# Key, query and feature projections of a linear attention layer on 64-row halves of TensorE, in a two-layer kernel

## The chip, the cores and the metric

The kernel runs on one NeuronCore of a Trainium2 chip. The metric is the device time of one execution in microseconds (us); lower is better. A profile is one profiled execution, with a record of every instruction of the engines: TensorE (PE, its weight loads as PEld), VectorE (DVE), ScalarE (ACT), GpSimd (POOL) and SyncE (SP), and of the DMA queues.

## The reference

Linear attention with exponential features, followed by a gated MLP with a spatial mixing matrix. Batch 8, 8 heads, 576 tokens, head dimension 64, 128 features (256 with both signs), model width 512, 1024 hidden.

```python
def phi(x):
    proj = np.einsum('bhsd,df->bhsf', x, w_phi)
    proj = proj - np.max(np.abs(proj), axis=-1, keepdims=True)
    return np.concatenate([np.exp(proj), np.exp(-proj)], axis=-1)
q_p, k_p = phi(q), phi(k)
kv = np.einsum('bhsf,bhsd->bhfd', k_p, v)
z = np.sum(k_p, axis=2)
num = np.einsum('bhsf,bhfd->bhsd', q_p, kv)
den = np.einsum('bhsf,bhf->bhs', q_p, z)[..., None] + 1e-06
x = (num / den)            # then tokens x (heads * head_dim)
h = np.maximum(x @ w_in, 0.0)
u, v = h[..., :512], h[..., 512:]
v_n = (v - mean(v)) / np.sqrt(var(v) + 1e-06)
v_s = np.einsum('ts,bsd->btd', w_spatial, v_n) + b_spatial[None, :, None]
out = (u * v_s) @ w_out
```

## The kernel before

**Units.** Of each batch's 576 tokens, 512 are handled as four blocks of 128 and the last 64 as a tail. A *pair* unit is two heads of one batch (8 blocks of 128 tokens by 64 dimensions); a *tail* unit is the 64 last tokens of all heads for two batches. There are 36 units, numbered `i` from 0: four pair units a batch, and one tail unit for each two batches (units 1, 9, 18 and 27). Batches 2 to 7 begin at units 10, 14, 19, 23, 28 and 32.

**What a unit needs.** The transposed inputs `kT` and `qT` have 128 partitions: two blocks of 64 dimensions on top of each other, so four columns groups `j` with two blocks each. For the first batches TensorE transposes them (L225); from batch 2 on SP does it by DMA for a whole batch (`cross`, tiles `kT_b` and `qT_b`). The weight `wphi2` is 128 x 256 with w_phi in rows 0 to 63 of its left half and again in rows 64 to 127 of its right half, zeros elsewhere.

- `by_token` (L229 to 234) projects: one matmul of 256 columns gives two blocks, since the zeros of `wphi2` keep them apart. `a_keys` reduces to the absolute maximum `mk` on DVE (L244) and evacuates exp(p) and exp(-p) into `kf` on ACT (L247). `a_queries` takes only the maxima `mq` (L258), which POOL (DVE in the first five units) splits into a high and a low bf16 part, `mhl`.
- `a_scale` makes exp(-mk) and exp(mk) (`em`, ACT L267) and POOL multiplies v by them (`vs`, L272).
- `a_max_t` transposes `mhl` on TensorE and DVE copies 16 rows to `mT` (L294).
- `a_qfeat` (L296 to 322) projects q once more with features on the partitions (L304), subtracts the maxima by a matmul with `sel`, a matrix of -1 (L308), and ACT evacuates exp(p) and exp(-p) into `qf` (L321). For tail units the two lines are L313 and L315.
- `a_kv` sums `kf` times `vs` over tokens (L334, L336), `a_num` multiplies `qf` by the sums (L354) and `norm` divides (L344, L345), giving `x`. `tail_num` does it for tails (L382), with 64 output columns of the array. `a_x_t` transposes `x` into `xT`, by DMA from SP for most units (L363).

**The gMLP.** When a batch's last unit is through, `b_tasks` puts its matrix products into `queue`: `b_v` (L403, evacuated by ACT, statistics on DVE), `b_ln` (normalizing on POOL, L413 to L420), `b_u` (L456), `b_s` (L477, L478), `b_o` (L500, with the store by SP). A task is four or five matmuls of 512 columns, and its cost is given in us.

**The order.** It is written out by hand. `step(i)` goes through `ORDER`, and each entry works on the unit whose lag to the step is listed; after each entry `fill` adds `RATE` times the entry's share to a credit (at most `CAP`) and takes tasks from the queue as long as half the next one's cost is covered. Before: keys and queries of unit i, attention of unit i-3, sums of unit i-2, inputs of unit i+1, features of unit i-2, `x` of unit i-4, maxima of unit i-1. The shares sum to 1.0 and `RATE` is 3.12. After each step come the loads and DMA transposes that `at` lists: k five steps ahead of a batch's first unit and q and v four steps ahead, `cross` two steps ahead (`AT, AB, XP = 4, 5, 2`). What is left in the queue after the last step is run then.

All PSUM tiles share one pool of 8 banks, and a framework sets the banks and the semaphores.

Of the kernel before, what the change touches and what calls it, by code (L numbers as in the profile page):

```python
# [8 lines left out]
FP32 = mybir.dt.float32  # L9
BF16 = mybir.dt.bfloat16  # L10
AF = mybir.ActivationFunctionType
# [5 lines left out]
def kernel(  # L17
# [42 lines left out]
    def pin(start):  # L60
        return lambda *a, **kw: tc.keep_in_program_order(start(*a, **kw))
# [72 lines left out]
    for i in range(NM):  # L134
        for tiles, name in ((mhl, "mhl"), (mT, "mT")):
# [1 line left out]
            pin(nc.vector.memset)(t, 0.0)  # L137
            tiles.append(t)

    sel1 = cpool.tile([P, H], BF16)  # L140
    sel = cpool.tile([P, H, F], BF16)
    pin(nc.vector.tensor_tensor)(out=sel1, in0=ident[:, 0:H], in1=ident[:, H:2 * H], op=ALU.add)
    pin(nc.vector.tensor_scalar)(out=sel, in0=sel1.unsqueeze(2).to_broadcast([P, H, F]), scalar1=-1.0,
                                 scalar2=None, op0=ALU.mult)
    for x in ("k", "q"):
        pin(nc.vector.tensor_copy)(out=st[0][x][:, 0:2], in_=first[x])
# [79 lines left out]
            u[x + "T"] = a1.tile([P, 4, P], BF16, tag=x + "T", name=x + "T", bufs=2 if x == "k" else 4)  # L226
            copy(out=u[x + "T"], in_=pt)

    def by_token(xT, half):  # L229
        ps = psum.tile([P, 4, F], FP32, tag="bank", name="ps")  # L230
        for x in range(2):
            nc.tensor.matmul(out=ps[:, 2 * x:2 * x + 2, :], lhsT=xT[:, 2 * half + x, :], rhs=wphi2,  # L232
                             start=True, stop=True)
        return ps

    def a_keys(u):

        u["mk"] = small.tile([P, H], FP32, tag="mk", name="mk")
        u["kf"] = feat.tile([P, 2, H, F], BF16, tag="kf" if u["pair"] else "kf_t", name="kf",
                            bufs=4 if u["pair"] else 2)  # L240
        for half in range(2):
            pk = by_token(u["kT"], half)
            hs = slice(4 * half, 4 * half + 4)
            nc.vector.tensor_reduce(out=u["mk"][:, hs], in_=pk, axis=AX.X, op=ALU.max,  # L244
                                    apply_absolute_value=True)
            for s, sc in ((0, 1.0), (1, -1.0)):
                nc.scalar.activation(out=u["kf"][:, s, hs, :], in_=pk, func=AF.Exp, bias=0.0, scale=sc)  # L247

    def a_queries(u):

        m, early = mhl[u["i"] % NM], u["i"] < EARLY
        if not early:
            mq = small.tile([P, H], FP32, tag="mq", name="mq")
        for half in range(2):
            pq = by_token(u["qT"], half)
            if early and half == 0:
                mq = pq[:, 0, 0:H]
            nc.vector.tensor_reduce(out=mq[:, 4 * half:4 * half + 4], in_=pq, axis=AX.X, op=ALU.max,  # L258
                                    apply_absolute_value=True)
        eng = nc.vector if early else nc.gpsimd  # L260
        eng.tensor_copy(out=m[:, 0:H], in_=mq)
        eng.tensor_tensor(out=m[:, H:2 * H], in0=mq, in1=m[:, 0:H], op=ALU.subtract)

    def a_scale(u):
        em = small.tile([P, 2, H], FP32, tag="em" if u["pair"] else "em_t", name="em", bufs=3 if u["pair"] else 1)
# [25 lines left out]
    def a_max_t(u):  # L291
        pt = psum.tile([P, P], BF16, tag="bank", name="pt")
        nc.tensor.transpose(out=pt, in_=mhl[u["i"] % NM], identity=ident)
        nc.vector.tensor_copy(out=mT[u["i"] % NM][0:2 * H, :], in_=pt[0:2 * H, :])  # L294

    def a_qfeat(u):  # L296

        m = mT[u["i"] % NM]
        u["qf"] = []
        for half in range(2):  # L300
            pq = psum.tile([P, 4, P], FP32, tag="bank", name="pq")
            if u["pair"]:
                for par in range(2):
                    nc.tensor.matmul(out=pq[:, 2 * par:2 * par + 2, :], lhsT=wphi2[:, par * F:(par + 1) * F],  # L304
                                     rhs=u["qT"][:, 2 * half:2 * half + 2, :], start=True, stop=False)
                    for x in range(2):
                        j = 4 * half + 2 * x + par
                        nc.tensor.matmul(out=pq[:, 2 * par + x, :], lhsT=sel[:, j, :], rhs=m,  # L308
                                         start=False, stop=(x == 1))
            else:  # L310
                for x in range(4):
                    h = 4 * half + x
                    nc.tensor.matmul(out=pq[:, x, :], lhsT=wphi2[:, (h % 2) * F:(h % 2 + 1) * F],  # L313
                                     rhs=u["qT"][:, h // 2, :], start=True, stop=False)
                    nc.tensor.matmul(out=pq[:, x, :], lhsT=sel[:, h, :], rhs=m, start=False, stop=True)  # L315
            if u["pair"]:
                qf = feat.tile([P, 2, 4, P], BF16, tag="qf", name="qf", bufs=7)
            else:
                qf = feat.tile([P, 2, 4, P], BF16, tag="qf_t", name="qf_t", bufs=4)
            for s, sc in ((0, 1.0), (1, -1.0)):  # L320
                nc.scalar.activation(out=qf[:, s], in_=pq, func=AF.Exp, bias=0.0, scale=sc)  # L321
            u["qf"].append(qf)

    def a_kv(u):
        d, dg, bl = st[u["b"]], gs[u["g"]], u["b"] % 2
# [21 lines left out]
    def a_num(u):  # L347
        d = st[u["b"]]
        u["x"] = a1.tile([P, NB, 2, D], BF16, tag="x", name="x", bufs=3)
        for hh in range(2):  # L350
            pn = psum.tile([P, NB, DA], FP32, tag="bank", name="pn")
            for pos in range(NB):
                for s in range(2):
                    nc.tensor.matmul(out=pn[:, pos, :], lhsT=u["qf"][hh][:, s, pos, :],  # L354
                                     rhs=d["kv"][:, 2 * u["pj"] + hh, s, :], start=(s == 0), stop=(s == 1))
            norm(pn, u["x"][:, :, hh, :])

# [13 lines left out]
    def tail_num(g, bls):  # L371
        d = gs[g]
        qf = d["unit"]["qf"]
        if "xt" not in d:
            d["xt"] = a1.tile([P, H, D], BF16, tag="xt", name="xt")
        for i in range(2):
            pn = psum.tile([P, 4, DA], FP32, tag="bank", name="pn")
            for y in range(4):
                for bl in bls:
                    r = slice(bl * TL, (bl + 1) * TL)  # L380
                    for s in range(2):
                        nc.tensor.matmul(out=pn[r, y, :], lhsT=qf[i][:, s, y, r],  # L382
                                         rhs=st[2 * g + bl]["kv"][:, 4 * i + y, s, :],
                                         start=(s == 0), stop=(s == 1))
            r = slice(bls[0] * TL, (bls[-1] + 1) * TL)
            norm(pn, d["xt"][r, 4 * i:4 * i + 4, :], r)
# [142 lines left out]
    def unit(i):  # L529
        return units[i] if 0 <= i < NU else None  # L530
# [3 lines left out]
    def b_tasks(b):  # L534
# [15 lines left out]
        if tail:  # L550
# [5 lines left out]
            for x in bls:  # L556
                ts += [(mm, lambda j=j, x=x: b_o(2 * g + x, j)) for j in range(NB)]
        return ts

    ORDER = (("keys", 0.375), ("queries", 0.25), ("attention", 0), ("sums", 0.25),  # L560
             ("next", 0.125), ("features", 0), ("out", 0), ("maxima", 0))
    RATE = 3.12
    CAP = 2.11
    LAGS = dict(next=-1, maxima=1, features=2, sums=2, attention=3, out=4)
    FIRST = dict(next=-1, maxima=1, features=2, sums=2, attention=3, out=3)
    credit = [0.0]

    def fill(share):
# [3 lines left out]
            task()  # L572
            credit[0] -= cost

    FT = dict(next=-1, maxima=1, features=2)

    def lag(u, what):
        return (FT if u["i"] == 1 else FIRST if u["pair"] and u["b"] == 0 else LAGS).get(what, 0)

    def step(i):  # L580

        if i == 0:
            a_transpose(units[0])
        for what, share in ORDER:
            for u in units[max(0, i - 5):i + 2]:
                if u["i"] + lag(u, what) != i or (what in ("sums", "attention", "out") and not u["pair"]):
                    continue
                last = u["pair"] and u["pj"] == NP - 1
                if what == "keys":
                    a_keys(u)  # L590
                    a_scale(u)
                elif what == "sums":
                    a_kv(u)
                elif what == "queries":
                    a_queries(u)
                elif what == "next":
                    a_transpose(u)
                elif what == "maxima":
                    a_max_t(u)
                elif what == "out":  # L600
                    a_x_t(u)
                    if last:
                        finish_batch(u, tail_x_t)
                        queue.extend(b_tasks(u["b"]))
                elif what == "features":
                    a_qfeat(u)
                elif what == "attention":
                    a_num(u)
                    if last:
                        finish_batch(u, tail_num)  # L610
            fill(share)

    def finish_batch(u, f):
        g, bl = u["g"], u["b"] % 2
        if g in SPLIT:
            f(g, [bl])
        elif bl == 1:
            f(g, [0, 1])
# [65 lines left out]
```

## Time and profile before

| what | value |
|---|---|
| median of 8 runs | 292.56 us (287.19 to 295.39) |
| the profiled execution | 291.43 us |
| its span, first to last instruction | 289.6 us |
| granted TensorE clock | 0.993 |
| PE busy (L334 and L354, 512 matmuls each, 66 columns) | 264.1 us, 91% |
| ACT busy (kf 144 and qf 144 instructions of 128x512) | 229.4 us, 79% |
| DVE busy | 201.9 us, 70% |
| POOL busy | 181.8 us, 63% |
| DMA | 40.31 MB, mean 139 GB/s |

How to read it: busy time is the union of an engine's instructions, so overlapping ones count once. The duration of a matmul is modelled and reaches into the next one's; the distance between the starts of two of them is what one costs. A group line gives the source line, engine, operation, tiles (out<-in) and shape, the count, busy us and mean ns of one, and after the second bar the idle time of the engine before these instructions and what ended it. A slice row cuts the span into 40 equal parts with the busy share of each in tenths.

### The profile page before, as it was taken

What the parts mean: (1) busy time and instruction counts of PE and PEld (TensorE: products, weight loads), DVE (VectorE), ACT (ScalarE), POOL (GpSimd) and SP (SyncE); (2) the same over time, 40 slices, a digit from 0 to 9 for tenths busy, and PEclk for the clock granted to TensorE, in tenths of its full rate; (3) what the DMA queues carried; (4) which work ended last, traced back from release to release, by engine and by line L of the source; (5) the groups of instructions that cost most, each with busy time, mean ns of one, the idle gap of its engine ahead of it and who ended that gap; (6) DMA issues with size and microseconds to landing.
All of it is one profiled execution on the core that took longest, in us unless ns stands there. A gap on an engine that the chain in (4) does not pass through costs nothing.

```text
span 289.6 us, 7965 instructions
## 1 busy us (share of the span) xinstructions
PE 264.1 (91%) x3070; PEld 179.4 (62%) x3070; DVE 201.9 (70%) x509; ACT 229.4 (79%) x517; POOL 181.8 (63%) x320
## 2 busy tenths in 40 slices
PE   3188899999999999889999999989999999999984
PEld 2067676776766766557667677656677777545441
DVE  6289997968868697377696987568697854454610
ACT  7658998899799988599999779789999756566033
POOL 8349998896337996748689964844969700058300
PEclk9999999999999999979999999999999999999999
DMA  7979999948377699997974999999311003600037
GB/s 202 225 126 158 210 232 206 173 141 107 48 169 155 180 149 127 168 242 157 119 122 91 215 131 157 228 301 247 57 22 20 18 2 91 238 3 0 0 85 243
DMA packets 81706, 40.31 MB, mean 139 GB/s; under 512 B 50242, under 2 KB 77058, under 8 KB 81668
## 3 DMA queue, kind: packets, MB, share of 16 engines
q1 hardware_dynamic: 54180, 28.32, 44.3%
q0 software_dynamic: 27328, 11.41, 34.7%
q8 instruction: 24, 0.39, 0.6%
q14 instruction: 14, 0.11, 0.1%
q10 hardware_dynamic: 160, 0.07, 0.1%
HBM read 32.85 MB, written 9.44 MB: 146 GB/s over the span
## 4 chain that ended last, share of the span: by engine, by line
PE 58%; ACT 16%; DVE 11%; DMA 10%; POOL 2%; issue 2%; ACTq 0%; SPq 0%; POOLq 0%; DVEq 0%
PE pv L403 10%; PE ps L477 8%; PE pu L456 7%; PE po L500 6%; ACT qf L321 5%; DMA out_dram<-ob 5%; ACT kf L247 5%; PE ps L232 5%; PE pv L334 4%; PE pn L354 4%; DMA q_tl<-in_q_dram 4%; PE pq L308 3%; PE pq L304 3%; DVE mk L244 3%; ACT ob L502 2%; PE ps L478 2%
## 5 line engine op out<-in xcount | busy, mean ns | idle before, releaser
L247 ACT ACTIVATE kf<-ps 128x512 bf16<-128x512 f32 x144 | 77.2, 680 | 6.7 <-DVE mk L244 6.5
L272 POOL TENSOR_TENSOR vs<-v_f,em 128x512 bf16<-128x512 f32 x64 | 65.5, 1047 | 22.5 <-ACT em L267 21.6
L321 ACT ACTIVATE qf<-pq 128x512 bf16<-128x512 f32 x128 | 67.9, 665 | 8.5 <-PE pq L308 8.5
L244 DVE TENSOR_REDUCE mk<-ps 128x4 f32<-128x512 f32 x72 | 46.1, 677 | 0.7 <-PE ps L232 0.2
L258 DVE TENSOR_REDUCE mq<-ps 128x4 f32<-128x512 f32 x62 | 39.9, 680 | 4.0 <-PE ps L232 2.6
L502 ACT COPY ob<-po 128x512 f32<-128x512 f32 (+1 forms) x37 | 21.7, 606 | 23.9 <-PE po L500 16.2
L406 DVE BATCH_NORM_STATS2 stats<-vr 128x6 f32<-128x512 bf16 (+1 forms) x37 | 24.8, 688 | 20.2 <-ACT vr L405 20.0
L477 PE MATMUL ps<-w_spT,vn 128*128 128x512 bf16 x128 | 32.8, 379 | 0.0
L403 PE MATMUL pv<-w_in_bf,xT 128*128 128x512 bf16 x128 | 32.0, 386 | 0.5 <-DVE mT L294 0.5
L456 PE MATMUL pu<-xT,w_in_bf 128*128 128x512 bf16 x128 | 31.5, 379 | 0.0
L480 DVE TENSOR_TENSOR uT<-ps,uT 128x512 bf16<-128x512 f32 x32 | 22.0, 688 | 12.7 <-PE ps L478 11.5
L500 PE MATMUL po<-w_out_bf,uT 128*128 128x512 bf16 x128 | 30.4, 379 | 0.0
L308 PE MATMUL pq<-mT,sel 128*128 128x128 bf16 x256 | 30.0, 219 | 0.0
L308 PEld LDWEIGHTS <-sel 128*128 128x128 bf16 x256 | 25.0, 98 | 3.9
L405 ACT ACTIVATE vr<-pv 128x512 bf16<-128x512 f32 (+1 forms) x37 | 22.8, 672 | 4.2 <-PE pv L403 4.1
L354 PEld LDWEIGHTS <-qf 128*128 128x128 bf16 x512 | 20.8, 98 | 8.5 <-issue 1.9
L345 DVE TENSOR_TENSOR x<-pn,rc 128x256 bf16<-128x256 f32 x64 | 25.0, 418 | 0.5
L334 PE MATMUL pv<-vs,kf 128*128 128x66 bf16 x512 | 24.9, 195 | 0.2 <-ACT kf L247 0.2
L420 POOL TENSOR_SCALAR vn<-vr,rs 128x512 bf16<-128x512 bf16 x32 | 24.2, 773 | 0.8
L354 PE MATMUL pn<-kv,qf 128*128 128x66 bf16 x512 | 22.7, 195 | 1.3 <-ACT qf L321 1.2
L334 PEld LDWEIGHTS <-kf 128*128 128x128 bf16 x512 | 22.1, 98 | 1.8 <-issue 1.0
L304 PE MATMUL pq<-qT_b,wphi 128*128 128x256 bf16 x96 | 22.4, 273 | 0.0
(120 smaller groups left out, 530.2 us busy)
## 6 DMA issues: line engine op xcount, KB each, us to landing
v_f<-in_v_dram SPq DMA_DIRECT2D x8, 1024.0 KB, 8.6
out_dram<-ob SPq DMA_DIRECT2D x32, 256.0 KB, 4.0
k_bf<-in_k_dram POOLq DMA_DIRECT2D x7, 512.0 KB, 7.3
q_bf<-in_q_dram POOLq DMA_DIRECT2D x7, 512.0 KB, 8.2
v_tl<-in_v_dram SPq DMA_DIRECT2D x8, 128.0 KB, 6.6
w_in_bf<-in_moe_w_in_dram POOLq DMA_DIRECT2D x2, 512.0 KB, 7.9
out_dram<-ob SPq DMA_DIRECT2D x8, 128.0 KB, 2.4
k_tl<-in_k_dram POOLq DMA_DIRECT2D x8, 64.0 KB, 6.7
```

Of the source, the lines that this page charges most:

```text
L244: nc.vector.tensor_reduce(out=u["mk"][:, hs], in_=pk, axis=AX.X, op=ALU.max, apply_absolute_value=True)
L247: nc.scalar.activation(out=u["kf"][:, s, hs, :], in_=pk, func=AF.Exp, bias=0.0, scale=sc)
L258: nc.vector.tensor_reduce(out=mq[:, 4 * half:4 * half + 4], in_=pq, axis=AX.X, op=ALU.max, apply_absolute_value=True)
L272: nc.gpsimd.tensor_tensor(out=vs[:, s, :, 0:D], in0=st[u["b"]]["v"][:, pj * H:(pj + 1) * H, :], in1=em[:, s, :].unsqueeze(2).to_broadcast( ...
L308: nc.tensor.matmul(out=pq[:, 2 * par + x, :], lhsT=sel[:, j, :], rhs=m, start=False, stop=(x == 1))
L321: nc.scalar.activation(out=qf[:, s], in_=pq, func=AF.Exp, bias=0.0, scale=sc)
L334: nc.tensor.matmul(out=pv[:, hh, s, :], lhsT=u["kf"][:, s, 4 * hh + c, :], rhs=u["vs"][:, s, 4 * hh + c, :], start=(c == 0), stop=False)
L354: nc.tensor.matmul(out=pn[:, pos, :], lhsT=u["qf"][hh][:, s, pos, :], rhs=d["kv"][:, 2 * u["pj"] + hh, s, :], start=(s == 0), stop=(s == 1))
L403: nc.tensor.matmul(out=pv[r], lhsT=lhs(kc), rhs=w_in_bf[:, kc, HALF:DFF], start=(kc == 0), stop=(kc == KC - 1))
L456: nc.tensor.matmul(out=pu, lhsT=w_in_bf[:, kc, dc * P:(dc + 1) * P], rhs=d["xT"][:, kc, :], start=(kc == 0), stop=(kc == KC - 1))
L477: nc.tensor.matmul(out=ps, lhsT=d["vn"][:, sp, cs], rhs=w_spT[:, sp, 0:T0], start=(sp == 0), stop=False)
L500: nc.tensor.matmul(out=po[r], lhsT=lhs(dc), rhs=w_out_bf[:, dc, :], start=(dc == 0), stop=(dc == KC - 1))
```

## The change

Each 256-column matmul with zeros in its weights becomes two matmuls of 128 columns that contract over 64 rows each: one on rows 0 to 63 and one on rows 64 to 127, issued in turn and written to two different PSUM banks. So `pk`, `pq` and the features `pf` of a unit take two banks each, one for even and one for odd blocks (`par`), rather than one bank for each half of the unit's blocks. The same holds for the features: one product of 512 columns for each half, then four of 128 columns for each half that subtract the maxima, now with the 64 rows of `sel` and `mT` in both halves (`mhl` carries its 16 columns twice, 64 apart; `mT` gets 80 rows).

`step` issues keys' and queries' projections of unit i and the features' of unit i-2 at its start, ahead of all else, and the reduces and evacuations as separate entries behind them. `ORDER`, `RATE` and `CAP` change. The entry "pk" has a share of the filler, so gMLP tasks may stand between "pk" and "pq". The loads' lead is as before. The lines from 334 on keep their numbers; others move (the projections are L241, the features L249 and L254, kf L268, mk L264, mq L276, vs L292, mT L314; qf stays L321).

```diff
-    sel1 = cpool.tile([P, H], BF16)
+    sel1 = cpool.tile([P, 2, H], BF16)
...
+    def a_project(u, x):
+        u["p" + x] = [psum.tile([P, 4, F], FP32, tag="bank", name="ps") for par in range(2)]
+        for j in range(4):
+            for par in range(2):
+                r = rows_of(par)
+                nc.tensor.matmul(out=u["p" + x][par][:, j, :], lhsT=u[x + "T"][r, j, :],
+                                 rhs=wphi2[r, par * F:(par + 1) * F], start=True, stop=True)
+
+    def a_features(u):
+        m = mT[u["i"] % NM]
+        u["pf"] = [psum.tile([P, 4, P], FP32, tag="bank", name="pf") for par in range(2)]
+        for par in range(2):
+            r = rows_of(par)
+            nc.tensor.matmul(out=u["pf"][par], lhsT=wphi2[r, par * F:(par + 1) * F], rhs=u["qT"][r],
+                             start=True, stop=False)
+        for j in range(4):
+            for par in range(2):
+                r = rows_of(par)
+                nc.tensor.matmul(out=u["pf"][par][:, j, :], lhsT=sel[r, 2 * j + par, :], rhs=m[r, :],
+                                 start=False, stop=(j == 3))
...
+        nc.vector.tensor_reduce(out=u["mk"].rearrange("p (j two) -> p j two", two=2)[:, :, par], in_=pk, axis=AX.X,
+                                op=ALU.max, apply_absolute_value=True)
+        for s, sc in ((0, 1.0), (1, -1.0)):
+            out = u["kf"][:, s].rearrange("p (j two) f -> p j two f", two=2)[:, :, par, :]
+            nc.scalar.activation(out=out, in_=pk, func=AF.Exp, bias=0.0, scale=sc)
...
-        nc.vector.tensor_copy(out=mT[u["i"] % NM][0:2 * H, :], in_=pt[0:2 * H, :])
+        nc.vector.tensor_copy(out=mT[u["i"] % NM][0:D + 2 * H, :], in_=pt[0:D + 2 * H, :])
...
-                    nc.tensor.matmul(out=pn[:, pos, :], lhsT=u["qf"][hh][:, s, pos, :],
+                    nc.tensor.matmul(out=pn[:, pos, :], lhsT=u["qf"][pos // 2][:, s, 2 * hh + pos % 2, :],
...
-    ORDER = (("keys", 0.375), ("queries", 0.25), ("attention", 0), ("sums", 0.25),
-             ("next", 0.125), ("features", 0), ("out", 0), ("maxima", 0))
-    RATE = 3.12
-    CAP = 2.11
-    LAGS = dict(next=-1, maxima=1, features=2, sums=2, attention=3, out=4)
+    ORDER = (("pk", 0.25), ("pq", 0), ("pf", 0), ("keys0", 0),
+             ("queries", 0), ("keys1", 0.25), ("feat0", 0), ("attention", 0.125), ("next", 0.125), ("sums", 0), ("feat1", 0), ("maxima", 0), ("out", 0))
+    RATE = 3.25
+    CAP = 1.66
+    LAGS = dict(next=-1, maxima=1, sums=2, attention=3, out=4)
```

## The prediction

> **What bounds the kernel now.** Read first the busy shares and the slices of the page, then the windows by stage, then the timeline of TensorE in one step.
>
> ```profile
> PE 264.1 (91%) x3070; PEld 179.4 (62%) x3070; DVE 201.9 (70%) x509; ACT 229.4 (79%) x517; POOL 181.8 (63%) x320
> ...
> PE   3188899999999999889999999989999999999984
> ...
> L247 ACT ACTIVATE kf<-ps 128x512 bf16<-128x512 f32 x144 | 77.2, 680 | 6.7 <-DVE mk L244 6.5
> ```
>
> TensorE is dense from slice 7 to the end, but its busy time overlaps: one 128x512 matmul lasts 379 ns and the next starts after 216. So I count by the distance between starts, which the timeline shows:
>
> ```profile
> 151.69 0.66 PE L354 MATMUL pn<-kv,qf 128*128 128x66 bf16 x16
> 152.20 0.29 PE L334 MATMUL pv<-vs,kf 128*128 128x66 bf16 x4
> ...
> 152.82 1.02 PE L456 MATMUL pu<-xT,w_in_bf 128*128 128x512 bf16 x4
> 153.69 1.06 PE L468 MATMUL pu<-xTt,w_in_bf 128*128 128x128 bf16 x16
> 154.58 0.27 PE L304 MATMUL pq<-qT_b,wphi 128*128 128x256 bf16 x1
> 154.69 0.27 PE L308 MATMUL pq<-mT,sel 128*128 128x128 bf16 x2
> ```
>
> Four 512-column products take 0.87 (152.82 to 153.69), sixteen of 128 columns 0.89, sixteen of 66 columns 0.51: 0.216, 0.056 and 0.032 each, whether or not new weights are loaded. A 256-column product takes 0.11. The same count on ScalarE: its 128x512 instructions last 680 but four of them span 2.07 us in the timeline, so one every 0.478; em takes 0.10, kv 0.26. DVE: a reduce every 0.60.
>
> Three stages follow. Start: to 48.1 us, where unit 8's keys are projected. Steps: units 8 to 34, 48.1 to 225.1, 27 steps of 6.56. Drain: 225.1 to 289.6, nearly all gMLP products.
>
> ```profile
> 20.00:35.00 15.00, 12.22 (x198) 10.40 (x198) 14.18 (x41) 14.09 (x35) 14.85 (x21) 1.00 1.08 161
> ...
> 48.10:226.60 178.50, 173.48 (x2121) 121.57 (x2120) 137.28 (x338) 159.69 (x375) 127.83 (x232) 0.99 0.90 147
> ```
>
> In these window lines (PE, PEld, DVE, ACT, POOL, clock, DMA share, GB/s) the start belongs to DVE, ACT and POOL, not to TensorE. In the steps I sum distances between starts over the order of instructions: TensorE 166 of 177 us (163.4 and 27 mode switches, below), ACT 152 (27 x 4.28 for features and scales, the rest evacuations), POOL 135 (two vs products a step at 1.0 each, normalizing at 0.75, some 0.85 for a DMA issue), DVE 128. TensorE bounds, ACT is close behind. The larger of TensorE and ACT, step by step, sums to 167.8; the stage took 177.0, so coupling and waits cost 5.5%.
>
> **The change, part by part.**
>
> *Halves.* Before, a unit's key and query projections are 8 products of 256 columns (0.87) and its features 0.88 (154.58 to 155.46). After, the same columns stand in 64-row products: 4 pairs of 128 for keys, 4 for queries, for features one pair of 512 and 4 of 128. If a pair takes the time of one: 12 x 0.056 + 0.216 = 0.89. Saved 0.87 a unit, 23.6 in the 27 steps. No 64-row pair is in the trace. Bounds: nothing saved, or all. The nearest rows are the tail products, which use 64 columns of the array; in batches 0 and 1 one half alone, later both alternately:
>
> ```profile
> 42.48 0.70 PE L382 MATMUL pn<-kv,qf_t 128*64 128x66 bf16 x16
> 43.14 0.30 PE L334 MATMUL pv<-vs,kf 128*128 128x66 bf16 x4
> ...
> 134.56 0.71 PE L382 MATMUL pn<-kv,qf_t 128*64 128x66 bf16 x32
> 135.19 1.04 PE L456 MATMUL pu<-xT,w_in_bf 128*128 128x512 bf16 x4
> ```
>
> Sixteen in one half take 0.66, thirty-two in both 0.63: full doubling, between column halves. The Trainium skill (TensorE: Matmul & The Clock Gate, Measured speedup vs the span model) gives 3.07 for four row tiles, 77% of ideal. By it a burst is 0.89 / 0.77 = 1.16 and saves 0.60; TensorE in the steps would be 7 us fuller, still under ACT below. I take the row.
>
> *Switches.* The rule that speaks against the change: a change of tiling mode drains TensorE (TensorEngine Tiling (Array Packing), Key Properties); it gives no price. The row: into L382 the distance is 0.12 instead of 0.03, out of it the same, 0.095 lost at each. If a drain were the page's constant for a lone matmul, 166 ns (TensorE: Matmul & The Clock Gate, Single matmul latency), it would be 0.166. The order of instructions shows that it is not one burst: the filler after "pk" puts gMLP work between keys and queries in most steps, so a step has 4 switches. In the 27 steps there are 121 instead of 27: 11.5 us by the row (2.6 before), an estimated 20 by the rule. I take 11.5; with 20 TensorE reaches 142 and ties with ACT.
>
> *Filler.* A step gave credit 1.0 x 3.12 and gives 0.75 x 3.25 = 2.44 now. From the order of instructions at the starts above, gMLP work in the steps falls from 83.5 to 66.0, and that behind the last key projection rises from 49.9 to 67.4. ACT loses 19 evacuations (9.1 us) from the steps.
>
> Sum for the steps, TensorE: 163.4 - 23.6 - 17.5 = 122.3, with switches **133.8**; ACT **142.8** (8 x 0.478 for features, 0.2, 0.26, and 66 us worth of evacuations); POOL still **135**; DVE 121. ACT is the bound now, by little. The larger of TensorE and ACT by step sums to 146.2; with the same 5.5%, 154.2.
>
> *Moves.* The six banks at a step's start are two each of keys, queries, features. By the order with its waits, the banks of a key burst come from readers of the step before that are done early (a gMLP evacuation, an x product), so TensorE may lead ACT by most of a step: nothing beyond the 5.5%. If a key burst had to wait for the last feature evacuation instead, ACT would stand through a burst and a reduce, 0.2 + 0.7 a step, 25 us in all: the upper end. The loads stay at their steps, but steps get shorter. SP issues kT and qT at the end of step i-2, and they are used in step i:
>
> ```profile
> k_bf<-in_k_dram POOLq DMA_DIRECT2D x7, 512.0 KB, 7.3
> q_bf<-in_q_dram POOLq DMA_DIRECT2D x7, 512.0 KB, 8.2
> ...
> kT_b<-k_bf SPq DMA_TRANSPOSE x6, 7.9
> qT_b<-q_bf SPq DMA_TRANSPOSE x6, 4.5
> ```
>
> In the trace kT lands 0.4 to 6.5 us ahead of its use, qT 0 (twice) to 6.6. POOL issues the k load of batch 4 7.1 us after TensorE left step 14, as vs products and layer norm stand before it. One step shorter by 0.85 takes 0.9 from batch 3 (kT slack 0.4); four steps (3.4) less their slack take 1.5 from batch 4 and 1.0 from batch 6; three steps take 2.5 from batch 5's qT. That is 5.9; ACT has about half a step's backlog, so I charge half, 3.0. Between 0 and 17 (rival 1).
>
> *Drain.* +17.5 gMLP, +0.8 switches, -1.8 from the two units' features still there: **+16.5**. Dense before (window 226.6 to 245.2: TensorE busy 18.60 of 18.60), dense after.
>
> *Start.* TensorE is not the bound there: 0, between -1 (step 7, 7.7 us, has gMLP work) and +2.
>
> *At nothing:* one more small DVE operation for sel1 hides in the 0.9 us that DVE waits for the first load. mT copied over 80 partitions, not 16: the same 128 elements each. mhl writes 16 columns for 8: at most 10 ns on POOL (L274 with 32 columns takes 213 ns, L261 with 8 192). kf is now written in runs of 128 elements; no ACT row has such runs, DVE's x (runs of 64) is at its usual 418 ns: taken as nothing, at worst 10%, 7 us of ACT.
>
> **Sum.** Steps 154.2 + 3.0 - 177.0 = -19.8; drain +16.5; start 0: **-3.3**. The profiled execution took 291.43 us (span 289.6), so 288.1. The runs' median is 292.56, 1.1 above; in the same ratio the median after is **289**.
>
> **Rivals.**
> 1. *Late transposes (slower).* If POOL and SP keep their pace, batches 3 to 6 cannot start earlier than they do, and half of the 22.8 saved in the steps is waited away: -11.4 + 16.5 = +5, 297; if all six are held, +16.5, 309. TensorE works in order: a key projection that waits for kT holds queries, features and gMLP products behind it, and ACT runs dry half a step later. It decides once waits at batch starts exceed 6 us in sum. For: zero slack twice, POOL 135 of 154. Against: a waiting TensorE lets POOL catch up.
> 2. *Halves one after the other.* TensorE 133.8 + 23.6 = 157.4, with 5.5% 166: -11 + 16.5 + 1.5, 299. For: only column halves are seen side by side.
> 3. *ACT stays fed.* Where one engine leads clearly (steps 23 to 27: 30.8 of TensorE in 31.6) the loss is 2.6%. ACT 142.8 + 2.6% = 146.5: -30.5 + 16.5, 278; half way there 283. For: TensorE would have 9 us of slack against ACT and DVE 22, so either may be late without holding ACT up. Against: steps 28 to 34, where TensorE and ACT tie (41.9 and 41.2), took 45.0, 7.5% over.
>
> **Numbers.** Forecast 0.50 (284 to 294), rival 1 0.20, rival 2 0.08, rival 3 0.22. About 2% is what the measurement can tell: 286.7 and 298.4. Faster: rival 3 and a fifth of the forecast, 0.32; slower: most of rivals 1 and 2, 0.22; within 0.46. Cases of both signs have weight; the range 279 to 300 takes in rival 3's middle and the mild form of 1 and 2.
>
> **What would show it.** Pairs of L241 starting some ns apart, 0.056 from pair to pair; 0.1 lost at each border; steps near 5.8; ACT's idle time in the steps near 12 us; 81 us from the last key projection to the end. Wrong if the steps last 6.2 or more (waits on qT_b, kT_b or on banks), if L241 advances by 0.056 per product, or if kf's starts lie over 0.5 apart.

## The result and the profile after

The kernel became slower by 1.65%: median 295.04 us of 11 runs (292.05 to 300.79) against 291.26 of 32 runs before, ratio 1.0165 with a 95% interval of 1.0117 to 1.0213. Ratios compare undisturbed executions alone, so they are not exactly quotients of the medians; the profiled executions of e5_filler, e7_kv_dve, e10_twobursts and e11_before_loads, below, are disturbed ones.

From the page of after, the rows that answer to those of before: the shares, TensorE's slices, and the group of kf.

```profile
PE 249.5 (86%) x3270; PEld 152.0 (52%) x3270; DVE 203.5 (70%) x510; ACT 229.9 (79%) x517; POOL 181.6 (63%) x320
...
PE   3087788989999878899988999879989998999983
...
L268 ACT ACTIVATE kf<-ps 128x512 bf16<-128x512 f32 x144 | 80.0, 645 | 12.9 <-DVE mk L264 12.7
```

TensorE lost 14.6 us of busy time and its slices are looser, ACT has as much to do as before, and the time did not fall. The windows by stage (PE, PEld, DVE, ACT, POOL, clock, DMA share, GB/s) show why. The first is the steps, units 8 to 34; the other two are what follows the last key projection.

```profile
48.50:206.30 157.80, 142.38 (x2168) 90.53 (x2168) 129.32 (x316) 147.96 (x352) 115.06 (x209) 1.00 1.04 160
206.30:225.00 18.70, 17.41 (x255) 10.73 (x255) 11.15 (x33) 16.29 (x36) 8.58 (x16) 1.00 0.15 50
225.00:290.30 65.30, 59.20 (x375) 29.21 (x373) 25.11 (x54) 26.67 (x45) 19.82 (x36) 0.99 0.22 73
```

The steps take 157.9 instead of 177.0, the drain 84.0 instead of 64.5. In the steps the engine that is busy to 94% is ACT. The same from the traces of two executions of each kernel:

| us | before | before again | after | after again |
|---|---|---|---|---|
| device time | 291.43 | 290.14 | 292.05 | 295.15 |
| start | 48.1 | 50.0 | 48.5 | 49.6 |
| steps | 177.0 | 173.8 | 157.9 | 159.8 |
| drain | 64.5 | 64.6 | 84.0 | 84.0 |

The drain repeats to 0.1 us; start and steps vary by 1 to 3 us. The profiled execution of after is the fastest of its 11, that of e1_again lies at the median. So the cost at the medians is read from the first and the last column: start +1.5, steps -17.2, drain +19.5, sum +3.8.

### The profile page after: what moved, and what is told of

Same layout as the page of the kernel before. It is cut to its first block, busy times and chain, and to the rows that moved or that the text cites. A ratio compares the mean times of both kernels' runs of the same rounds, so it can differ in the third digit from the quotient of the medians.

```text
span 290.3 us, 8361 instructions
## 1 busy us (share of the span) xinstructions
PE 249.5 (86%) x3270; PEld 152.0 (52%) x3270; DVE 203.5 (70%) x510; ACT 229.9 (79%) x517; POOL 181.6 (63%) x320
## 4 chain that ended last, share of the span: by engine, by line
PE 38%; ACT 25%; DMA 16%; POOL 11%; DVE 5%; issue 3%; SPq 1%; POOLq 0%; ACTq 0%; DVEq 0%
PE po L500 9%; ACT qf L321 9%; ACT kf L268 8%; PE ps L477 7%; DMA q_tl<-in_q_dram 6%; PE pv L403 5%; PE pu L456 5%; DMA qT_b<-q_bf 4%; POOL vs L292 4%; DMA q_bf<-in_q_dram 3%; PE ps L241 3%; ACT uT L458 2%; ACT vr L405 2%; DMA v_f<-in_v_dram 2%; ACT ob L502 2%
## 5 line engine op out<-in xcount | busy, mean ns | idle before, releaser
L268 ACT ACTIVATE kf<-ps 128x512 bf16<-128x512 f32 x144 | 80.0, 645 | 12.9 <-DVE mk L264 12.7
L321 ACT ACTIVATE qf<-pf 128x512 bf16<-128x512 f32 x144 | 86.9, 680 | 3.7 <-PE pf L254 3.6
L292 POOL TENSOR_TENSOR vs<-v_f,em 128x512 bf16<-128x512 f32 x64 | 65.6, 1043 | 23.0 <-ACT em L287 22.8
L264 DVE TENSOR_REDUCE mk<-ps 128x4 f32<-128x512 f32 x72 | 47.6, 681 | 6.1 <-PE ps L241 4.1
L502 ACT COPY ob<-po 128x512 f32<-128x512 f32 (+1 forms) x37 | 22.7, 617 | 26.9 <-PE po L500 24.1
L276 DVE TENSOR_REDUCE mq<-ps 128x4 f32<-128x512 f32 x62 | 40.2, 680 | 5.4 <-PE ps L241 4.8
L406 DVE BATCH_NORM_STATS2 stats<-vr 128x6 f32<-128x512 bf16 (+1 forms) x37 | 25.5, 689 | 21.5 <-ACT vr L405 21.1
L405 ACT ACTIVATE vr<-pv 128x512 bf16<-128x512 f32 (+1 forms) x37 | 25.5, 690 | 6.2 <-PE pv L403 4.1
L334 PEld LDWEIGHTS <-kf 128*128 128x128 bf16 x512 | 23.4, 99 | 6.2 <-ACT kf L268 0.7
L345 DVE TENSOR_TENSOR x<-pn,rc 128x256 bf16<-128x256 f32 x64 | 25.8, 418 | 1.0
L458 ACT ACTIVATE uT<-pu 128x512 bf16<-128x512 f32 x32 | 20.3, 634 | 4.2 <-PE pu L456 4.2
L413 POOL TENSOR_SCALAR var<-mv 128x4 f32<-128x4 f32 x8 | 1.9, 239 | 33.5 <-DVE mv L407 28.5
L336 PE MATMUL pv<-vst,kf 128*128 128x66 bf16 x128 | 21.5, 193 | 0.0
```

The source lines that it names most:

```text
L264: nc.vector.tensor_reduce(out=u["mk"].rearrange("p (j two) -> p j two", two=2)[:, :, par], in_=pk, axis=AX.X, op=ALU.max, apply_absolute_v ...
L268: nc.scalar.activation(out=out, in_=pk, func=AF.Exp, bias=0.0, scale=sc)
L276: nc.vector.tensor_reduce(out=mq.rearrange("p (par j) -> p par j", par=2)[:, par], in_=u["pq"][par], axis=AX.X, op=ALU.max, apply_absolute ...
L292: nc.gpsimd.tensor_tensor(out=vs[:, s, :, 0:D], in0=st[u["b"]]["v"][:, pj * H:(pj + 1) * H, :], in1=em[:, s, :].unsqueeze(2).to_broadcast( ...
L321: nc.scalar.activation(out=qf[:, s], in_=u["pf"][par], func=AF.Exp, bias=0.0, scale=sc)
L334: nc.tensor.matmul(out=pv[:, hh, s, :], lhsT=u["kf"][:, s, 4 * hh + c, :], rhs=u["vs"][:, s, 4 * hh + c, :], start=(c == 0), stop=False)
```

## The experiments

### Both kernels once more

e1_again is the changed kernel, e12_before_again the one before, both without an edit.

> The changed kernel once more, for a second profiled execution. Theory 'given back': the steps stage (unit 8 to the last key projection) is again near 158 us and the drain near 84, and the whole stays 1 to 2% above the kernel before. Rival 'late transfers': the execution profiled first was a short one; this one shows longer steps, 160 to 164, with waits on qT_b, kT_b or q_tl of 8 us or more where the first had 6.5.

> The kernel before once more, for a second profiled execution. If the start (to unit 8) of the changed kernel is really longer, this one shows 48 again, against 48.5 to 52 in seven executions of the changed kernel's variants; if the start only varies with the first loads, it lies anywhere in 48 to 52 here too. Steps 175 to 179, drain 64.5.

e1_again: 295.22 us, ratio 1.0278 (1.0206 to 1.035). e12_before_again, one run: 290.14. Their stages stand in the table.

The traces also show what no list of waits does. In e1_again TensorE stood 2.22 us for the queries of batch 4, as in after (its row stands below, at 116.92), and then had half its clock for 3.4 us. First the four products behind that stand in e1_again, then the same four in after, then the window of e1_again, whose clock (the third number from the end) is 0.50:

```profile
118.23 1.89 PE L477 MATMUL ps<-w_spT,vn 128*128 128x512 bf16 x4
...
117.69 1.04 PE L477 MATMUL ps<-w_spT,vn 128*128 128x512 bf16 x4
...
118.20:121.60 3.40, 3.40 (x26) 1.77 (x23) 2.56 (x7) 3.21 (x8) 1.42 (x4) 0.50 0.85 254
```

After kept a clock of 1.00 there. By an estimate 3.4 us at half the clock hold 1.7 us of work, so at most 1.7 are lost. Such a stretch also lies in the steps of before (125.3 to 128.7), e4, e9, e11, e17 and e19; e7 and e13 have two, e6, e10 and e16 one of 6.8, e5 one of 10.3. Each follows or spans a stand of TensorE of 1.5 us or more, but after and e2_fullrows have stands of 2.2 us and more without one, so what decides stays open. e12, e14 and e15 have none in their steps. A difference of under 2 us between two single traces can thus be such a stretch.

### Do two halves run side by side?

e2_fullrows keeps the order, the filler and the two banks, and lets every product contract over all 128 rows again, the zeros of `wphi2` keeping blocks apart.

```diff
-  lhsT=u[x + "T"][r, j, :], rhs=wphi2[r, par * F:(par + 1) * F]
+  lhsT=u[x + "T"][:, j, :], rhs=wphi2[:, par * F:(par + 1) * F]
...
-  lhsT=wphi2[r, par * F:(par + 1) * F], rhs=u["qT"][r]
+  lhsT=wphi2[:, par * F:(par + 1) * F], rhs=u["qT"]
...
-  lhsT=sel[r, 2 * j + par, :], rhs=m[r, :]
+  lhsT=sel[:, 2 * j + par, :], rhs=m
...
-  nc.vector.tensor_copy(out=mT[u["i"] % NM][0:D + 2 * H, :], in_=pt[0:D + 2 * H, :])
+  nc.vector.tensor_copy(out=mT[u["i"] % NM][0:2 * H, :], in_=pt[0:2 * H, :])
```

> The changed order, banks and filler, but every projection contracts over all 128 rows (the zeros of wphi2 and of mT keep blocks apart), so no two run side by side and no mode changes. TensorE in the steps: 122.3 + 23.6 + 2.2 for 23 switches = 148, ACT 143. If the halves carry the shorter steps: steps 163 to 168, drain about 85, in all 299 to 304. If TensorE has slack and ACT or waits set the steps: within 2 us of the changed kernel, about 295.

299.18 us, ratio 1.0387 (1.0191 to 1.0583): 4.0 us more than e1_again beside it. TensorE's timeline of after first, then that of e2_fullrows.

```profile
121.14 0.40 PE L241 MATMUL ps<-wphi,kT_b 64*128 64x128 bf16 x8
121.47 0.29 PE L489 MATMUL ps<-w_spT,vn 128*128 128x64 bf16 x4
...
122.03 0.19 PE L491 MATMUL ps<-w_spT,vnt 128*128 128x64 bf16 x1
122.16 0.40 PE L241 MATMUL ps<-wphi,qT_b 64*128 64x128 bf16 x8
122.39 0.38 PE L249 MATMUL pf<-qT,wphi 64*128 64x512 bf16 x2
122.61 0.39 PE L254 MATMUL pf<-mT,sel 64*128 64x128 bf16 x8
```

```profile
137.17 0.61 PE L241 MATMUL ps<-wphi,qT_b 128*128 128x128 bf16 x8
137.61 0.59 PE L249 MATMUL pf<-qT_b,wphi 128*128 128x512 bf16 x2
138.05 0.61 PE L254 MATMUL pf<-mT,sel 128*128 128x128 bf16 x8
138.49 1.03 PE L403 MATMUL pv<-w_in_bf,xT 128*128 128x512 bf16 x4
```

Eight products of 64 rows take 0.23 (122.16 to 122.39), two of 512 columns 0.22; with 128 rows the same columns take 0.44. The two starts of a pair lie 4 ns apart at the median (most of them 3 or 4) and the next pair most often follows after 0.056. The switches show too: 0.33 from the keys' burst to L489, which is 0.22 and 0.10, and 0.13 from L491 into the queries' burst where the line before it took 0.03. Halving the products is worth 2.8 us of steps (162.6 against 159.8 of e1_again) to 4.7 (against 157.9 of after, which like e2_fullrows has no stretch at half the clock), not the estimated 14.7 by which it empties TensorE (23.6 less 0.095 for each of the 94 switches that e2_fullrows does without): TensorE isn't the bound there.

### Late transposes

e14_after_onecross and e15_before_onecross leave out the ten DMA transposes of batches 3 to 7, whose units then read those of batch 2 (so their keys and queries are another batch's). The same edit in both kernels; it also takes the transposes' traffic away.

```diff
     def cross(b):
+        if b > 2:
+            d["kT"], d["qT"] = st[2]["kT"], st[2]["qT"]
+            return
```

> The changed kernel with the DMA transposes of batch 2 used for batches 3 to 7 too (ten transposes and the waits on k and q loads ahead of them are left out; the loads themselves stay). Theory 'late transfers': the waits on qT_b and kT_b (4 to 6 us) go and the steps shorten by at least as much, to 151 to 154; in all 287 to 290. Theory 'the steps are set by ACT and the banks': steps 157 to 159, in all 293 to 295.

> The kernel before with the same ten transposes left out. Both theories: TensorE is the bound, so little goes: the 2 us of waits on qT_b and some of the wait on a store (5 us, behind the transposes in SP's queue), steps 171 to 176, in all 286 to 290. If the changed kernel gains clearly more than this one from it, late transfers are what the shorter steps run into.

e14: 289.22 us, ratio 0.9992 (0.9964 to 1.0019). e15: 288.86, ratio 0.9963 (0.9939 to 0.9988). Without transposes the change costs nothing and brings nothing: start 49.6 and 50.0, steps 172.8 and 152.7, drain 64.6 and 84.0 (before, after), in sum -0.3. With them it loses 1.65%. So of the 1.65%, about 1.4 points (1.73 of after less 0.37 of before) go with the transposes and their traffic, which this edit doesn't separate. Where they wait shows in TensorE's timeline of after, all rows that a load or a transpose held up within the steps:

```profile
107.32 0.38 PE L227 MATMUL pt<-ident,q_tl 128*128 128x128 bf16 x4 [1.72 <-DMA q_tl<-in_q_dram]
...
116.92 0.40 PE L241 MATMUL ps<-wphi,qT_b 64*128 64x128 bf16 x8 [2.22 <-DMA qT_b<-q_bf]
...
188.57 0.40 PE L241 MATMUL ps<-wphi,kT_b 64*128 64x128 bf16 x8 [1.05 <-DMA kT_b<-k_bf]
...
191.72 0.40 PE L241 MATMUL ps<-wphi,qT_b 64*128 64x128 bf16 x8 [1.48 <-DMA qT_b<-q_bf]
```

Together 6.5 us, of batches 4 and 7. In e1_again rows of this kind come to 5.5, of batches 4, 6 and 7, and one more of batch 7 is put down to ACT (1.63 at 194.75) though its qT_b landed at 194.70: 7.2. Batch 4 is late because its loads meet: before, the v load (96.9 to 103.1) was all but through when POOL issued k (102.1 to 108.8); after, k (91.7 to 102.1), v (93.0 to 104.8) and q (100.2 to 111.5) overlap, and each takes 3 to 6 us more than before.

Before has the same trouble in another place, seen in ACT's timeline of before:

```profile
123.17 0.59 ACT L502 COPY ob<-po 128x512 f32<-128x512 f32 x1 [3.47 <-DMA out_dram<-ob]
...
186.31 0.59 ACT L502 COPY ob<-po 128x512 f32<-128x512 f32 x1 [1.50 <-DMA out_dram<-ob]
```

ACT waits 5.0 us for a store buffer. SP issues stores and transposes in one order; for the first wait its timeline of before shows why:

```profile
108.86 6.52 SPq L61 DMA_TRANSPOSE kT_b<-k_bf  x1
115.63 2.89 SPq L61 DMA_TRANSPOSE qT_b<-q_bf  x1
118.61 0.54 SPq L514 DMA_DIRECT2D out_dram<-ob  x1
```

The copy into that store's buffer began at 111.2 and took 0.6; the store itself was issued only at 118.6, behind the transposes. For the second wait nothing of the kind shows: SP issued the stores from 179.0 on, right behind their copies (from 178.3 on).

e4_loads issues all loads and transposes one step earlier.

```diff
-    AT, AB, XP = 4, 5, 2
+    AT, AB, XP = 5, 6, 3
```

> The changed kernel with every load and transpose one step earlier (AT, AB, XP = 5, 6, 3). Theory 'late transfers': the waits on qT_b, kT_b and q_tl in the steps (5 to 6.5 us in two executions) go, and what ACT or the banks do not take back shortens the steps, to 153 to 156; in all 289 to 292. Theory 'ACT sets the steps': TensorE waits elsewhere instead, steps 157 to 159, in all 293 to 295.

293.08 us, ratio 1.0125 (1.0039 to 1.021), steps 157.2. The waits of batch 7 went, that of batch 4's queries grew from 2.22 to 3.43 us: k's transpose is issued at 101.1 and lands at 113.5, q's load takes from 93.9 to 110.7. Issuing earlier did not help where the transfers meet.

### More filler in the steps

e5_filler raises the credit until the steps hold as much gMLP work as before (83.5 us, 49.9 behind). e17_onecross_filler does the same on top of e14.

```diff
-    RATE = 3.25
-    CAP = 1.66
+    RATE = 4.15
+    CAP = 2.11
```

> The changed kernel with RATE 4.15 and CAP 2.11, which puts the gMLP work back as before: 83.5 us in the steps, 49.9 behind. TensorE in the steps 139.8 + 12 = 152, ACT 152. Theory 'given back by the filler': drain about 66, steps 162 to 166, in all 277 to 282. Rival 'the steps are full': each us of gMLP work put back lengthens the steps by as much, 173 to 176 steps, in all 289 to 293.

> The transposes of batch 2 for all later batches, as in e14, and the gMLP work put back into the steps (RATE 4.15, CAP 2.11: 83.5 us there, 49.9 behind). Drain 65. If late transposes and the stores that queue behind them were what the filler ran into: TensorE and ACT both 152 in the steps, 160 to 165 there, in all 275 to 281. If the burst order itself couples TensorE, DVE and ACT so that more gMLP work does not fit: steps 169 to 174, in all 284 to 290.

e5: 297.43 us, ratio 1.0266 (1.0103 to 1.0429). Drain 64.2, but steps 181.5; the row of ACT's timeline that a single step of 17 us goes back to, and the load that SP issued just ahead of the store in question:

```profile
197.38 0.59 ACT L502 COPY ob<-po 128x512 f32<-128x512 f32 x1 [10.03 <-DMA out_dram<-ob]
...
184.21 0.53 SPq L61 DMA_DIRECT2D v_f<-in_v_dram  x1
```

This store was not held by a transpose of keys or queries: it was issued at 184.8, when the transposes of batch 6 had landed (by 181.3) and those of batch 7 were not yet issued, and it landed at 197.3, just after the v load ahead of it (1 MB, 196.2). In before, e12, e15 and e17, too, the store that SP issues behind this v load lands 0.7 to 1.1 us after it. TensorE's clock was 0.50 from 190.6 to 200.9. How often it costs so much stays open. e17, without transposes, is the cleaner case: 287.63 us, ratio 0.9881 (0.9792 to 0.9969); drain 64.4 (-19.6 against e14), steps 170.6 (+17.9). What is moved out of the drain comes back in the steps almost whole. Against e15, which has the same filler, the halves and their order bring 2.2 us of steps, and up to 1.7 more if e17's stretch at half the clock is set aside.

e3_oldorder keeps the halves and takes the order, rate and filler of before: each burst ahead of its own readers, 178 switches in the steps.

```diff
+    ORDER = (("pk", 0), ("keys0", 0), ("keys1", 0.375), ("pq", 0), ("queries", 0.25), ("attention", 0),
+             ("sums", 0.25), ("next", 0.125), ("pf", 0), ("feat0", 0), ("feat1", 0), ("out", 0), ("maxima", 0))
+    RATE = 3.12
+    CAP = 2.11
```

> Halves side by side, but in the order, RATE and CAP of before: three bursts a step (178 mode switches in the steps), gMLP work split as before (83.5 in the steps, 49.9 behind). Theory 'given back by the filler': drain back to about 67 us; TensorE in the steps 139.8 + 16.9 = 157, ACT 152, with 5.5 to 8% lost 166 to 170; start 48: in all 282 to 287, faster than before. Rival 'the burst is what feeds ACT': steps 175 or more as ACT waits for features at the end of a step, in all 290 or more.

290.04 us, ratio 1.0022 (0.9972 to 1.0072); steps 172.2, drain 63.8. Halves in the old order are worth nothing that can be measured. Beside it, in the same comparison, the new order with its filler took 295.22 with halves (e1_again) and 299.18 without (e2_fullrows): with the transposes in place, the loss belongs to the new order and its cut filler, not to the halves. e10_twobursts has this order with `out` and `maxima` ahead of the features (so that keys of the next step join their burst: 126 switches), loads one step earlier and a fifth store buffer.

> A version meant to beat both: halves in the order, RATE and CAP of before, with the feature products moved to the end of the step, where they meet the next step's key products (126 switches in the steps instead of 178), loads one step earlier and a fifth store buffer. TensorE in the steps 139.8 + 12 = 152, ACT 152. If the halves' gain holds: steps 163 to 168, drain 65, in all 278 to 284. If waits between engines take it back: 288 to 292, as with three bursts.

294.8 us, median of 6 runs (288.99 to 297.05) without an interval, steps 175.4, with 6.8 us at half the clock and 4.3 in which ACT waits for stores: no gain is shown, but whether the 52 saved switches brought anything stays open.

### Is it ACT's load?

e7_kv_dve takes the evacuation of kv from ACT to DVE in all units; e19_onecross_filler_kv does it on top of e17.

```diff
-        copy = nc.vector.tensor_copy if u["i"] < EARLY else nc.scalar.copy
+        copy = nc.vector.tensor_copy
```

> The changed kernel with all kv copies on DVE instead of ACT: in the steps 27 x 0.26 = 6 us less on ACT and about 8 us more on DVE (129 us busy of 158 so far). Theory 'ACT sets the steps': steps 152 to 155, in all 289 to 292. Rival 'waits between engines set them': 295 to 298, as DVE's queue delays mk and with it kf.

> The change without the ten later transposes and with the filler of before (RATE 4.15, CAP 2.11), which took 287.6 us with steps of 170.6, and here with the sums kv evacuated by DVE in all units, which takes some 6.3 us from ACT. Outputs of batches 3 to 7 are not the reference's. Theory A (with the filler back, TensorE at 151 and ACT at 152 tie, and the tie costs the steps 12%): steps 165 to 168, total 282 to 285. Theory B (the order decides: ACT waits for mk at each step's start however much it has to do): steps 169 to 172, total 286 to 289, ACT idle up from 12.9 to 18 or more.

e7: 294.02 us, ratio 1.0062 (1.0021 to 1.0103). ACT has 141.7 us in the steps instead of the 147.9 of e1_again, its idle time rose from 11.9 to 18.3, and the steps took 160.0 (159.8). These steps hold two stretches at half the clock where those of e1_again hold one, so up to 1.7 us of gain could hide. The interval of the ratio lies under that of the change alone, and the medians of all runs lie 1.0 us apart (294.02, 295.04): a gain of 0.3 to 1% is likely. e19 is the cleaner case: 289.19 us, ratio 0.9985 (0.9959 to 1.001), steps 172.3: not faster than e17 at all. Below, ACT's largest wait within the steps, from the waits of e14, e17 and e19 in this order (in these kernels lines stand 3 further down, so L271 is kf):

```profile
ACT kf L271 <- DVE mk L267: 3.5, 5, 1.7
```

```profile
ACT kf L271 <- DVE mk L267: 6.8, 10, 0.9
```

```profile
ACT kf L271 <- DVE mk L267: 13.7, 16, 1.6
```

With 5.5 us less to do ACT waits 6.9 us more for the key maxima. So with the filler back it is not ACT's load alone that sets the length of a step; the chain at its start (banks, key burst, reduce, then kf) is the likely cause. But the edit gives the copies to DVE, which makes the maxima (busy 142.1 in the steps of e19, 136.9 in e17), so a later mk may be the edit's own doing, and no run takes load from ACT without giving it to DVE. e14 is another case: ACT is idle 5.4 of 152.7 us there.

### One burst for all three

e6_oneburst moves the filler's share from behind "pk" to behind "pf" (76 switches in the steps instead of 121), e18_onecross_oneburst does so on top of e14. e9_all joins e4, e5, e6 and e7 with a fifth store buffer.

```diff
-    ORDER = (("pk", 0.25), ("pq", 0), ("pf", 0), ("keys0", 0),
+    ORDER = (("pk", 0), ("pq", 0), ("pf", 0.25), ("keys0", 0),
```

> The changed kernel with the filler's share moved from behind the key products to behind the feature products: one burst of 26 products a step, 76 mode switches in the steps instead of 119 (4 us of TensorE less). Theory 'ACT sets the steps': ACT has 94% of them, so within 2 us of the changed kernel, 293 to 297. Rival 'switches and TensorE count': 4 us shorter, 290 to 292. It can also lengthen, if ACT has nothing to do while the burst runs ahead of the gMLP work: its waits for mk then grow from 6 us.

> The change with batches 3 to 7 reading batch 2's transposed keys and queries (ten transposes of SP left out, so the outputs of those batches are not the reference's), and keys, queries and features in one burst: the filler's share moves from behind 'pk' to behind 'pf' (76 instead of 121 switches in the steps). Without the burst's move this kernel took 289.2 us, steps 152.7; with the transposes and the one burst 303.0, steps 165. Theory A (the one burst lost by making late transposes worse): steps near 152 or less, 4 us of switches having gone, total 285 to 290, ACT waits for mk under 3 us. Theory B (the order itself loses: queries and features ahead of the filler hold the maxima and key features back): steps 157 to 162, total 294 to 299, ACT waits for mk 6 to 10 us.

> Everything together: one burst, loads a step earlier, kv on DVE, a fifth store buffer, and the gMLP work back as before (83.5 us in the steps, 49.9 behind). TensorE in the steps 139.8 + 7.8 = 148, ACT about 146. If ACT's load, late transfers and stores set the steps: 158 to 163, drain 65, in all 273 to 279. If the steps are full whatever is in them: 170 or more, in all 285 or more.

e6: 302.97 us, ratio 1.0455 (1.0334 to 1.0577), steps 165.0. e18: 293.86 us, ratio 1.0142 (1.0052 to 1.0231), steps 157.9. So one burst loses 5.1 us of steps by its order alone, against e14, although it saves 45 switches of 0.095; ACT's wait for mk within the steps is 7.2 where e14 has 3.5, TensorE waits 4.1 where e14 has 0.7 for banks of pf, most of them held by gMLP evacuations, and 2.9 where e14 has 0.2 for uTt. e6 is 9.1 us above e18, as after is 5.8 above e14: that goes with the transposes, and e6's steps have 6.8 us at half the clock. e9: 293.59, ratio 1.0142 (1.0028 to 1.0257); ACT waits 17.4 us for mk in the steps, and TensorE stood 5.3 us for one xT, whose DMA transpose SP issued behind those of keys and queries.

### The drain

e13_otail_later runs the tail's output task four tasks before the last output of its pair of batches rather than first of them, so that DVE's uTt is older when TensorE reads it.

```diff
-            ts.append((mm, lambda: b_o_tail(g, bls)))
...
+            ts.insert(len(ts) - 4, (mm, lambda: b_o_tail(g, bls)))
```

> The changed kernel with the tail's last product moved behind the first output products of the two batches, so that TensorE has work while DVE finishes uTt. The drain holds this wait twice (1.02 us each), where the kernel before has one in the drain and two in the steps. If the drain's extra 3 us are such waits: drain 82 instead of 84, in all 292 to 294. If TensorE only waits elsewhere: drain 84.

294.23 us, ratio 1.0118 (1.009 to 1.0147). Drain 81.8, 2.2 less, while the steps of its profiled execution took 162.1, with waits for kT_b, qT_b and q_tl of 8.3 and two stretches at half the clock: in the total no gain is shown.

### The best of it

e16_loads_kv_otail joins e4, e7 and e13. e11_before_loads is the kernel before with loads a step earlier and a fifth store buffer, so that stores queue less.

```diff
-    ... tag="ob", name="ob", bufs=4)
+    ... tag="ob", name="ob", bufs=5)
...
-    AT, AB, XP = 4, 5, 2
+    AT, AB, XP = 5, 6, 3
```

> The changed kernel with earlier loads, kv on DVE and the tail's last product later. If the gains of the three add up (2, 1 and 2 us): 289 to 291. If what ACT is spared goes to the next late transfer, as in e7 alone: 292 to 294.

> The kernel before with loads and transposes one step earlier and a fifth store buffer. It had 0 to 2 us of waits on qT_b and 3 to 5 on a store: at best 2 to 3 us shorter, 287 to 289 (e15 without the transposes has 288.9). If earlier loads only move DMA traffic onto other transfers, as for batch 4 in e4: 290 to 292.

e16: 293.86 us, ratio 1.0107 (1.0043 to 1.0172). By its trace no load or transpose holds TensorE in the steps any more; instead ACT waits 6.3 us for one store that SP issued at 133.9, behind two transposes (from 121.0 on), and TensorE 5.8 with it. No run issues stores and transposes from different queues. e11: 288.27 us, ratio 0.9937 (0.9909 to 0.9966): the only kernel here that computes all and beats both, by 0.6%.

## Why the prediction was wrong

The forecast was -3.3; +3.8 came, at executions that lie at the medians. Its three stages against them (each of the two has one stretch at half the clock in its steps):

| us | forecast | measured |
|---|---|---|
| start | 0 | +1.5 |
| steps | -19.8 | -17.2 |
| drain | +16.5 | +19.5 |

**Right: halves, switches, ACT as the next bound.** Pairs run side by side at 0.056, a border costs 0.09 to 0.10, so TensorE fell as the sum had it, and rival 2 is out. The 77% that the prediction took from the Trainium skill (TensorE: Matmul & The Clock Gate, Measured speedup vs the span model), for four tiles of 32 rows, is not seen with these two of 64: 0.23 for what takes 0.44 is 96% of double. In a stretch of after without late transfers, 136 to 162 us, the chain by line is:

```profile
by line: ACT qf L321 29.8%; ACT kf L268 27.5%; ACT vr L405 10.7%; ACT uT L458 10.2%; issue 5.9%; DVE stats L406 5.3%; DVE mk L264 4.6%; ACT em L287 3.5%; ACT kv L339 2.1%; ACT kT L229 1.8%
```

It is ACT almost alone, as the sum of 142.8 against 133.8 said. Over all the steps of after it is not: qf and kf have 25.5% of that chain, and transfers of q and v 20.4%. Without transposes the steps take 152.7, where 154.2 was forecast.

**Failed: "dense before, dense after" (drain, 16.5).** It counted 17.5 us of moved products, 0.8 of switches and nothing else. By starts, TensorE loses 1.50 us beyond the price of its products in the drain of before and 5.03 in that of after, 0.76 of it switches; so 2.8 were left out of the sum, and 16.5 + 2.8 is 19.3. TensorE's timeline of after has these as its longest waits of the stage, and that of before the last line alone:

```profile
212.18 1.02 PE L403 MATMUL pv<-w_in_bf,xT 128*128 128x512 bf16 x4 [0.43 <-ACT vr L405]
...
218.12 0.40 PE L254 MATMUL pf<-mT,sel 64*128 64x128 bf16 x8 [0.73 <-DVE mT L314]
...
243.80 1.04 PE L500 MATMUL po<-w_out_bf,uTt 128*128 128x512 bf16 x4 [0.86 <-DVE uTt L495]
...
277.97 1.04 PE L500 MATMUL po<-w_out_bf,uTt 128*128 128x512 bf16 x4 [0.86 <-DVE uTt L495]
...
277.37 1.04 PE L500 MATMUL po<-w_out_bf,uTt 128*128 128x512 bf16 x4 [0.86 <-DVE uTt L495]
```

So one tail output more now stands where no other work covers DVE's uTt; e13 moved it and took 2.2 us off the drain. And pf comes in one piece right behind the transposed maxima, with DVE's copy to mT between them. The window of before that was read as dense (226.6 to 245.2) showed the state of a queue with other work between; the work that moved in brought its own waits.

**Failed: the late transposes (3.0 charged of 5.9).** They cost 5.2 us in the one execution of after and 7.1 in the one at the median (157.9 and 159.8 less 152.7; up to 1.7 of the latter by half the clock), about what the prediction had listed and then halved. It halved them since ACT has half a step's backlog. Most came through: ACT is idle 5.4 us of the steps of e14, 9.9 of after and 11.9 of e1_again, where TensorE waits 1.4, 6.5 and 7.2 for transfers. These waits are past the 6 us from which rival 1 was to decide; its mechanism is what happened, its size (165.6 us of steps) is not. Of the batches it named, 5 kept 1.4 to 2.8 us of slack; 4, put at 1.5, waited 2.2 and its tail's q 1.7, for a reason that was not in the sum, loads that meet; 7, which it did not name, waited 2.5. In e1_again 6 waited 1.4, put at 1.0.

**Only part of the base: 177.0.** It held waits of its own, 5.0 us of ACT for stores, 3.5 of them behind transposes, and 3.4 us at half the clock; a second execution, with 2.9 for stores and the full clock, took 173.8 and one without transposes 172.8. Where no transpose is late the steps go from 172.8 to 152.7, -20.1; without its late term the prediction had 177.0 to 154.2, -22.8. The factor of 5.5% carried part of these waits into the forecast, which is why its end, 157.2, was met: two errors that offset each other, so in part luck.

**Start.** 48.1 to 50.0 in three executions of before (49.6 the third, e15), 48.5 to 50.0 in three of after (e14 the third): no difference is shown, and +1.5 is what two single executions differ by, one of which has 3.4 us at half the clock there.

**What would have made it pay.** Rival 3 hoped for slack from a TensorE that is no longer the bound. Putting the gMLP work back to use that slack lengthens the steps by nearly what it takes out of the drain (e17, 17.9 of 19.6), and where ACT is relieved the wait for mk grows (e19). Which bank or reader holds that chain up in each step was not settled.

## What to carry to other kernels

Work that is moved out of a stage is not saved: when an engine gets lighter and the filler's rate is cut in the same edit, sum both stages, and look into the second for waits that the moved work brings along. When steps get shorter, list each transfer with its slack and charge what is missing in full unless the engine that sets the end shows idle time to absorb it; look also at which transfers will now run at the same time. A lighter engine pays only where a step waits for that engine. To find out, remove one load at a time and look at which wait grows, but do not hand the load to the engine that makes what is waited for. A stand of TensorE can cost more than its own length: look at the granted clock behind it.

## What the runs showed of the hardware

Two products over 64 rows each, on the two row halves, start 4 ns apart at the median and cost the time of one: 0.056 us for 128 columns, 0.22 for 512. Going into or out of that form costs 0.09 to 0.10 us. A DMA transpose of a batch's keys took 5.5 to 9.9 us to land in after and 12.5 in e4_loads, where it met loads; a q load there took 16.8 where the median of the page of after is 7.1. Such a transpose holds SP's queue while it is issued, 6.5 us of the 10.1 to its landing in before (at 108.9), and stores behind it are issued late: ACT waited 3.5 us for one in before and 6.3 in e16. A store that SP issued right behind a v load of 1 MB landed 0.7 to 1.1 us after that load in five traces; ACT waited 10.0 for one in e5_filler. The granted clock was 0.50 for 3.4 us behind a stand of TensorE of 2.22 us in e1_again, and stayed at 1.00 behind the same stand in after.
